# Attention and gated MLP on one core: the tenth and eleventh weighted products and row 15 change their places, and four marking matmuls are replaced by wider narrow halves

## The chip, the cores and the metric

The kernel runs on one core of a Trainium2 chip. The metric is the device time of one execution in microseconds (us); lower is better. A core has a matrix engine (TensorE, PE in the profile), VectorE (DVE), ScalarE (ACT), GpSimd (POOL) and SyncE (SP, which only issues transfers here), and 16 DMA engines. Each engine works off its own list of instructions in order, and waits at an instruction until the data and the buffers it needs are free.

## The reference

x is 2048 x 512. Both branches take the layer-normalised x.

```python
def attention(xn):                       # 32 heads of 16, window of 8 taps, 2 rows apart
    q, k, v = split(xn @ wqkv)
    idx = pos[:, None] - 2 * arange(8)   # rows before the first one are masked
    logits = einsum("bhsd,bhswd->bhsw", q, k[idx]) * 16 ** -0.5
    return einsum("bhsw,bhswd->bhsd", softmax(logits), v[idx]) @ wo

def gmlp(xn):
    z = gelu(xn @ w_in)                  # 2048 x 1792
    z1, z2 = z[:, :896], layernorm(z[:, 896:])
    g = w_sp @ z2 + b_sp                 # mixes the 2048 rows
    return (z1 * g) @ w_out

out = x + attention(xn) * silu(gmlp(xn))
```

Everything is 32-bit floating point.

## The kernel before

Every matrix product is made as three matmuls: each operand is split into a high part, rounded for the fast matmul type (on ScalarE, L195), and a low part, the rest (on VectorE, L197), and high x high, high x low and low x high are summed in a bank of PSUM. A *bank* holds 128 x 512 numbers; there are eight, given out in turn by `mm`.

The 2048 rows are 16 blocks of 128, called rows 0 to 15 below (NT = 16, HT = 8). The stages, in the order in which TensorE works on them:

- q, k and v; then z1 (gelu of the first half of the MLP, stored to memory);
- z2, from about 217 to 294.85 us: rows i and 8 + i are made together, each in two halves, h = 0 with 512 columns and h = 1, the *narrow half*, with 384 (`z2_half`). ScalarE applies the gelu as it empties the bank; VectorE makes the statistics (`z2_stats`, L742 to L745), GpSimd the inverse root and the shift `nmz`, ScalarE normalises (L754 in `z2_normal`) and the row is split into the large buffer `BIG`; `combine` (L767) makes sums and differences of rows i and 8 + i;
- the spatial product w_sp @ z2 by seven products of half the size instead of eight (Strassen's way), m1 to m7, each in two column groups a and b, of 8 steps over the rows (`block_product`, L825). A group accumulates in four banks `banks[a, f]`, shown as g_0_0 to g_0_3 and g_1_0 to g_1_3. Each step uses one block of w_sp as weights, wsp_0_0 to wsp_0_7 for the first product m1a, split in the same way into "h" and "l" parts. ScalarE *seeds* a bank with the bias before matmuls add to it (`seed`, L843);
- the output product b (7 x 3 matmuls of 512 columns for each of 16 rows), the product s of the attention with wo, and the end.

The banks that the seeds fill have to be written in full by a matmul first. The last eight halves of the z2 stage (rows 6, 14, 7 and 15) end in the banks of m1a and m1b; their narrow halves write 384 columns only. `second_seeds`, called after the third pair of steps of m1a, therefore sends four *marking* matmuls (L983), one into each of g_1_0 to g_1_3, whose results the seeds then overwrite.

Attention runs in VectorE's gaps: 16 units of two steps. A step has scores (`pr`, L573), their reduction (`lg`, L580), softmax (L594 to L614, the exponential on ScalarE at L606), the *weighted product* of the weights with v (`pv`, L620; pv_4_4 is unit 4, step 4, the tenth one, `sums_of[9]`), its folds (on GpSimd at L633, on VectorE at L638 and L639), a transpose (L646) and a store. These instructions form one line, in which each is kept behind the one before.

The order of each engine's list is set by a scheduler that plans with costs and priorities; attention has the lowest priority (LOW). `tc.add_manual_dep(x, y, NOSYNC, ...)` puts x behind y in the plan, without a wait at run time. `lows` and `highs` list the splits' low and high parts in the order in which the program makes them, so that `lows[-1]` is the latest one at that place of the program.

Of the kernel before, what the change touches and what calls it, by code (L numbers as in the profile page):

```python
# [13 lines left out]
AF = mybir.ActivationFunctionType  # L14
# [5 lines left out]
FH = F // 2  # L20
FQ = FH // 2
H, DH, W, DIL = 32, 16, 8, 2
NT = S // P
# [3 lines left out]
CT = 512  # L27
NC = S // CT
JC = NT // NC
HT = NT // 2  # L30
F3 = 3 * P
ODD = 3
# [20 lines left out]
NOSYNC = mybir.DependencyInfo(mybir.DependencyClass.NoSync, mybir.DependencyReason.DATA)  # L53
# [4 lines left out]
def kernel(  # L58
# [13 lines left out]
    nc = tc.nc  # L72
    pins = [True]
    lows, highs, sums_of = [], [], []

    def pin(ins):
        return tc.keep_in_program_order(ins) if pins[0] else ins
# [35 lines left out]
    mvz = const.tile([P, NT, 2], F32, name="mvz")  # L113
    nmz = const.tile([P, NT], F32, name="nmz")
# [5 lines left out]
    def xn_at(j):  # L120
        return planes[:, FB - KB :, j, 0], planes[:, FB - KB :, j, 1]

    def z2_at(j):
        return planes[:, :, j, 0], planes[:, :, j, 1]

    def half(i):
        return BIG[:, i * CT : (i + 1) * CT]
# [16 lines left out]
    def blocks(t, n=KB):  # L144
        return t.rearrange("p (k q) -> p k q", k=n)
# [9 lines left out]
    def mm(name):  # L155
        return ps.tile([P, 512], F32, tag=f"bank{next(turn)}", name=name)
# [3 lines left out]
    def weight_pair(name):  # L160
        i = next(slot)
        return (
            wts.tile([P, 512], F32R, tag=f"whi{i}", name=name + "h"),
            wts.tile([P, 512], F32R, tag=f"wlo{i}", name=name + "l"),
        )

    def fetch(src, n, name):
        raw = raws.tile([P, 512], F32, tag="raw", name=name + "r", bufs=RAW)
        pin(nc.sync.dma_start(raw[:, :n], src))
        return raw  # L170

    def side_pair(name):
        return [wts.tile([P, CT], F32R, tag=f"w{n}", name=name + n) for n in "hl"]

    def prep(src, n, name, raw=None, pair_=None):
        if raw is None:
            raw = fetch(src, n, name)
        hi, lo = pair_ or weight_pair(name)
        split(hi[:, :n], lo[:, :n], raw[:, :n])
        return hi, lo  # L180
# [13 lines left out]
    def split(hi, lo, src):  # L194
        first_ = pin(nc.scalar.activation(hi, src, AF.Copy))  # L195
        highs.append(first_)
        lows.append(pin(nc.vector.tensor_tensor(lo, src, hi.bitcast(F32), op=ALU.subtract)))  # L197
        return first_
# [48 lines left out]
    rows = {}  # L247
# [45 lines left out]
    first = []  # L293
# [230 lines left out]
    def t4(name, n=2):  # L524
        t = wide.tile([P, 2 * CT], F32, tag="t4", name=name, bufs=WIDE)
        return t.rearrange("p (i t) -> p i t", i=2)[:, :n]
# [168 lines left out]
    for f in range(FB):  # L695
        pair_ = side_pair("w1_last") if f == FB - 1 else None
        wh, wl = prep(w_in1[:, f, :], KB * P, f"w1_{f}", pair_=pair_)
        for c in range(NC):
            pz = mm(f"z1_{f}_{c}")
            for k in range(KB):  # L700
                cc = slice(k * P, (k + 1) * P)
                xh, xl = [planes[:, FB - KB + k, c * JC : (c + 1) * JC, a] for a in range(2)]
# [5 lines left out]
            zt = zp[:, c % 2]  # L708
# [8 lines left out]
    HALF = (slice(0, 512), slice(512, FH))  # L717
    WID = (512, FH - 512)
    w2 = {
        (k, h): prep(w_in2[:, k, HALF[h]], WID[h], f"w2_{k}_{h}")  # L720
        for h in range(2)
        for k in range(KB)
    }

    def z2_half(j, h, zt):
        xh, xl = xn_at(j)
        pz = mm(f"z2_{j}_{h}")[:, : WID[h]]
        for k in range(KB):
            wh, wl = [w[:, : WID[h]] for w in w2[k, h]]
            nc.tensor.matmul(pz, xh[:, k], wh, start=k == 0, stop=False)  # L730
            nc.tensor.matmul(pz, xh[:, k], wl, start=False, stop=False)  # L731
            nc.tensor.matmul(pz, xl[:, k], wh, start=False, stop=k == KB - 1)  # L732
        nc.scalar.activation(zt[:, HALF[h]], pz, AF.Gelu_apprx_tanh)  # L733

    def spatial_block(c, js):
        return prep(w_sp[c, js], CT, f"wsp_{c}_{js}")
# [14 lines left out]

    def z2_normal(j, zt, n):
        zh, zl = z2_at(j)
        nc.scalar.activation(zt, zt, AF.Identity, bias=nmz[:, j : j + 1], scale=mvz[:, j, 1:2])  # L754
        split(zh[:, :n], zl[:, :n], blocks(zt, FB)[:, :n])

    first_part, last_part = slice(0, F3), slice(FH - F3, FH)

# [19 lines left out]
    spatial = {(0, 0): early_pair}  # L778
    raw_z = {}
    for i in range(HT + 2):  # L780
        if i in (1, 3):
            raw_sums(1, HT - 2 + i // 2)
        if i < HT:
            raw_z[i] = [t4(f"zt_{j}").rearrange("p i t -> p (i t)")[:, :FH] for j in (i, HT + i)]
            for h in range(2):
                for j, zt in zip((i, HT + i), raw_z[i]):
                    z2_half(j, h, zt)
                if i == HT - 1 and h == 0:
                    spatial[0, 1] = spatial_block(0, 1)
        if i == 5:  # L790
            b_a = t4("b_a")
            nc.sync.dma_start(
                b_a, b_sp[0:2, :].rearrange("c t -> (c t)").unsqueeze(0).to_broadcast([P, 2 * CT])
            )
            biases = [[b_a[:, 0], b_a[:, 1]]]
        if 0 < i <= HT:
            z2_stats(i - 1, raw_z[i - 1])
        if i > 1:
            for j, zt, n in zip((i - 2, HT + i - 2), raw_z[i - 2], (ODD + 1, FB)):
                z2_normal(j, zt, n)  # L800
            combine(i - 2, raw_z[i - 2])
# [27 lines left out]
    def z2_block(j, f):  # L829
        return [planes[:, f, j, a] for a in range(2)]  # L830

    def z1_pair(c, f0, n):
        zl = t4(f"zl_{c}_{f0}", n)
        nc.sync.dma_start(zl, z1_d[f0 : f0 + n, c].rearrange("f p t -> p f t"))
        return zl

    banks = {}
    for n in range(8):
        a, f = n // 2 % 2, n // 4 * 2 + n % 2
        banks[a, f] = mm(f"g_{a}_{f}")  # L840

    def seed(a, f, src, scale=1.0):
        return nc.scalar.activation(banks[a, f], src, AF.Copy, scale=scale)  # L843
# [4 lines left out]
    def block_product(a, name, z, w, odd=None, start=False, stop=False, steps=()):  # L848
        for n, s0 in enumerate(range(0, HT, 2)):
            for s in (s0, s0 + 1):  # L850
                wp = w(s)
                for f in range(ODD):
                    three(banks[a, f], z(s, f), wp, start and s == 0, s == HT - 1, not start)
                if odd:
                    three(banks[a, ODD], odd(s), wp, False, s == HT - 1, True)
            for do in steps[n] if steps else ():
                do()

    def plain(a, c, r):
        def w(s):  # L860
            js = r * HT + s
            pair_ = spatial.get((2 * a + c, js)) or spatial_block(2 * a + c, js)
            if (a, c, js) == (0, 0, 6):
                tc.add_manual_dep(
                    sums_of[9].ins, lows[-1].ins.name, NOSYNC, reason="first weights ahead"
                )
            return pair_

        return w

    def summed(a, half_, i):
        return lambda s: prep(sums_d[a, half_, s, :, i], CT, f"ws_{a}{half_}{i}_{s}")
# [12 lines left out]
    def at(r, f0):  # L885
        return lambda s, f: z2_block(r * HT + s, f0 + f)
# [9 lines left out]
    def minus(out_, p_, q_):  # L896
        nc.vector.tensor_tensor(out_, p_, q_, op=ALU.subtract)
# [28 lines left out]
    def gated(c, f, src, zt):  # L926
        times(zt, src, zt)
        split(*ut_at(c, f), zt)
# [32 lines left out]
    def upper_last(a, f0, n):  # L961
        zl, yl = z1_pair(2 * a, LAST + f0, n), t4(f"yl_{a}_{f0}", n)
        nc.sync.dma_start(yl, y_d[a, f0 : f0 + n].rearrange("f p t -> p f t"))
        for f in range(f0, f0 + n):
            minus(yl[:, f - f0], banks[a, f], yl[:, f - f0])
            gated(2 * a, LAST + f, yl[:, f - f0], zl[:, f - f0])
# [12 lines left out]

    def second_seeds():  # L980
        for f in range(ODD + 1):

            nc.tensor.matmul(  # L983
                banks[1, f], z2_block(0, f)[0], half(0), start=True, stop=True
            )
        for f in range(ODD + 1):
            seed(1, f, biases[1][0])

    block_product(
# [62 lines left out]
    upper_last(0, 2, 1)  # L1052
    block_product(1, "m3b", at(1, LAST), summed(1, 1, 0))
    wout = [prep(w_out[:, f, :], D, f"wout_{f}") for f in range(FB)]
    upper_last(1, 0, 2)
    upper_last(1, 2, 1)
    for a in range(2):
# [14 lines left out]
    for i, j in enumerate(rows_of):  # L1072
        c, jj = divmod(j, JC)
# [104 lines left out]
```

## Time and profile before

| | us |
|---|---|
| median of 3 runs | 695.79 |
| lowest, highest | 694.64, 697.7 |
| the profiled execution | 694.39 |
| its span | 692.4 |
| busy in the span: PE | 686.6 |
| DVE | 619.5 |
| ACT | 278.6 |
| POOL | 214.0 |

The span is the part of the execution in which the engines' instructions lie; 2.0 us lie around it. In a timeline row stand the start, the duration, the engine, the line of the kernel, the operation, output <- inputs by the program's names with the numbers of buffers left out, the shape, and in brackets the idle time of the engine just before and what ended it. Matmuls overlap, so the distance of two starts tells what one costs.

### The profile page before, as it was taken

How to read it: one execution, taken by the hardware profiler on the slowest of the kernel's cores; microseconds unless marked ns; L12 is line 12 of the kernel's file. 1: busy time of each engine (PE TensorE's matmuls, PEld its weight loads, DVE VectorE, ACT ScalarE, POOL GpSimd, SP SyncE). 2: the span in 40 equal slices, each digit the busy share in tenths (PEclk: the TensorE clock that was granted, in tenths of full speed). 3: DMA queues.
4: the chain of work that ended last, by engine and by line, in shares of the span. 5: the costliest groups of instructions: out<-in, count | busy, mean ns of one | idle time of the engine just before them, and what ended most of it. 6: DMA issues, size and time to landing. Idle time of an engine off the chain costs nothing.

```text
span 692.4 us, 9239 instructions
## 1 busy us (share of the span) xinstructions
PE 686.6 (99%) x3084; PEld 573.6 (83%) x3084; DVE 619.5 (89%) x866; ACT 278.6 (40%) x458; POOL 214.0 (31%) x242
## 2 busy tenths in 40 slices
PE   8999999999999999999999999999999999999998
PEld 7788888888888899987888888888888888888886
DVE  6677867999999979899999999999999999979775
ACT  3343233324324256765624544433344353211531
POOL 3104737282343321223223221223201202632320
PEclk9999999999999999999999999999999999999999
DMA  8769899969999865266998778776585791645896
GB/s 268 245 199 297 276 353 370 344 213 336 411 410 384 334 222 186 92 216 218 287 401 299 277 241 294 228 251 223 161 290 196 234 339 65 214 159 191 251 324 238
DMA packets 102223, 182.36 MB, mean 263 GB/s; under 512 B 9184, under 2 KB 45280, under 8 KB 102176
## 3 DMA queue, kind: packets, MB, share of 16 engines
q1 hardware_dynamic: 56624, 102.21, 44.2%
q0 software_dynamic: 13824, 52.24, 20.9%
q10 hardware_dynamic: 31728, 27.33, 11.7%
q8 instruction: 24, 0.39, 0.2%
q14 instruction: 23, 0.19, 0.1%
HBM read 122.42 MB, written 59.32 MB: 262 GB/s over the span
## 4 chain that ended last, share of the span: by engine, by line
PE 93%; DVE 2%; DMA 1%; ACT 1%; issue 1%; POOL 1%; SPq 0%; DVEq 0%; ACTq 0%
PE g L825 37%; PE qkv L385 6%; PE qkv L387 6%; PE qkv L386 6%; PE z L705 4%; PE z L703 4%; PE b L1068 4%; PE b L1066 4%; PE b L1067 4%; PE z L704 4%; PE z L732 3%; PE z L731 3%; PE z L730 3%; PE s L1068 2%; PE s L1067 2%; PE s L1066 2%
## 5 line engine op out<-in xcount | busy, mean ns | idle before, releaser
L633 POOL TENSOR_TENSOR pv<-pv 128x1024 f32<-128x1024 f32 x29 | 69.6, 2401 | 92.8 <-DVE pv L620 82.5
L573 DVE TENSOR_TENSOR pr<-k,q 128x2048 f32<-128x2048 f32 x32 | 73.6, 2299 | 4.3 <-DMA k<-qkv_d 4.1
L620 DVE TENSOR_TENSOR pv<-v,lg 128x2048 f32<-128x2048 f32 x32 | 74.5, 2329 | 0.6
L580 DVE TENSOR_REDUCE lg<-pr 128x128 f32<-128x2048 f32 x32 | 72.9, 2279 | 0.1
L647 POOL DMA_DIRECT2D o_d<-tt x32 | 18.0, 563 | 137.8 <-DVE tt L646 104.6
L433 ACT ACTIVATE stage<-qkv 128x512 f32<-128x512 f32 x40 | 23.0, 590 | 30.9 <-DMA qkv_d<-stage 21.0
L1077 ACT ACTIVATE bt<-b 128x512 f32<-128x512 f32 x16 | 9.6, 599 | 50.0 <-PE b L1068 45.8
L807 POOL DMA_DIRECT2D ol<-o_d x32 | 17.8, 556 | 36.2 <-DMA ol<-o_d 9.1
L709 ACT ACTIVATE z1t<-z 128x512 f32<-128x512 f32 x28 | 15.5, 596 | 27.5 <-DMA z_d<-z1t 14.5
L732 PE MATMUL z<-w_0h,BIG 128*128 128x512 f32 x64 | 25.0, 391 | 0.0
L731 PE MATMUL z<-w_0l,BIG 128*128 128x512 f32 x64 | 25.0, 391 | 0.0
L730 PE MATMUL z<-w_0h,BIG 128*128 128x512 f32 x64 | 24.9, 389 | 0.0
L742 DVE BATCH_NORM_STATS2 zst<-zt 128x6 f32<-128x448 f32 x32 | 19.3, 613 | 6.1 <-ACT zt L733 6.0
L754 ACT ACTIVATE zt<-zt,nmz,mvz 128x896 f32<-128x896 f32 x16 | 17.5, 1129 | 17.1 <-POOL nmz L748 17.1
L280 DVE TENSOR_TENSOR xT<-xT,mr 128x512 f32<-128x512 f32 x20 | 13.8, 688 | 11.8 <-DMA mr<-mv_d 6.8
L638 DVE TENSOR_TENSOR pv<-pv 128x512 f32<-128x512 f32 x32 | 22.9, 715 | 0.0
L732 PE MATMUL z<-w_1h,BIG 128*128 128x384 f32 x64 | 21.5, 336 | 0.0
L730 PE MATMUL z<-w_1h,BIG 128*128 128x384 f32 x64 | 21.5, 335 | 0.0
L731 PE MATMUL z<-w_1l,BIG 128*128 128x384 f32 x64 | 21.4, 335 | 0.0
L733 ACT ACTIVATE zt<-z 128x512 f32<-128x512 f32 (+1 forms) x32 | 15.9, 536 | 13.5 <-DMA sums_d<-sa 10.2
L552 POOL DMA_DIRECT2D k<-qkv_d x13 | 7.0, 536 | 43.8 <-DVE pr L573 43.8
L393 POOL TENSOR_TENSOR sb<-sa,sb 128x512 f32<-128x512 f32 x12 | 18.9, 1574 | 5.1 <-DMA sb<-in_w_sp 4.8
(478 smaller groups left out, 2256.9 us busy)
## 6 DMA issues: line engine op xcount, KB each, us to landing
qkv_d<-stage ACTq DMA_DIRECT2D x24, 512.0 KB
v<-qkv_d POOLq DMA_DIRECT2D x14, 704.0 KB, 5.1
k<-qkv_d POOLq DMA_DIRECT2D x13, 704.0 KB, 5.8
sums_d<-sa POOLq DMA_DIRECT2D x14, 512.0 KB, 7.9
sums_d<-sb POOLq DMA_DIRECT2D x14, 512.0 KB, 7.9
z_d<-z1t ACTq DMA_DIRECT2D x14, 512.0 KB
zl<-z_d SPq DMA_DIRECT2D x12, 512.0 KB
tr<-t_d SPq DMA_DIRECT2D x12, 384.0 KB
```

The source lines that it names most:

```text
L385: nc.tensor.matmul(pq, xh[:, k], wh, start=k == 0, stop=False)
L386: nc.tensor.matmul(pq, xh[:, k], wl, start=False, stop=False)
L387: nc.tensor.matmul(pq, xl[:, k], wh, start=False, stop=k == KB - 1)
L573: line(nc.vector.tensor_tensor(pr, taps(ks[u], j0), qb.unsqueeze(1).to_broadcast([P, W, NJ * CS]), op=ALU.mult))
L580: line(nc.vector.tensor_reduce(lgs[u][:, j0 * HS : (j0 + NJ) * HS].rearrange("p i w -> p w i"), pr.rearrange("p w (i d) -> p w i d", d=DH) ...
L620: line(nc.vector.tensor_tensor(pv.rearrange("p w (i d) -> p w i d", d=DH), taps(vs[u], j0).rearrange("p w (i d) -> p w i d", d=DH), lgs[u] ...
L633: eng.tensor_tensor(pv[:, 0:4], pv[:, 0:4], pv[:, 4:8], op=ALU.add)
L730: nc.tensor.matmul(pz, xh[:, k], wh, start=k == 0, stop=False)
L731: nc.tensor.matmul(pz, xh[:, k], wl, start=False, stop=False)
L732: nc.tensor.matmul(pz, xl[:, k], wh, start=False, stop=k == KB - 1)
L825: nc.tensor.matmul(pg, z[a], w[b], start=start and i == 0, stop=stop and i == 2, skip_group_check=seeded)
L1066: nc.tensor.matmul(pp[:, cols], hi, wh, start=k == 0, stop=False)
```

## The change

1. The narrow half's first weight, w2_0_1, is loaded 512 columns wide, the last 512 of the 896. In rows 6, 7, 14 and 15 the first of a narrow half's twelve matmuls takes all of it and writes the whole bank, and the half's result lies in the bank's last 384 columns. The four marking matmuls go.
2. Row 15's normalisation is put behind row 7's high part.
3. The eleventh weighted product (`sums_of[10]`, pv_5_0) is put behind row 7's low part. The tenth, which was put behind the low part of weight row 6 (wsp_0_6), isn't held any more.
4. The twenty-fifth weighted product (`sums_of[24]`, pv_12_0) is put behind the low part of the last block of the output weights (wout_6).

```diff
     w2 = {
-        (k, h): prep(w_in2[:, k, HALF[h]], WID[h], f"w2_{k}_{h}")
+        (k, h): prep(
+            w_in2[:, k, slice(FH - CT, FH) if (k, h) == (0, 1) else HALF[h]],
+            CT if (k, h) == (0, 1) else WID[h],
+            f"w2_{k}_{h}",
+        )
         for h in range(2)
         for k in range(KB)
     }
     def z2_half(j, h, zt):
         xh, xl = xn_at(j)
-        pz = mm(f"z2_{j}_{h}")[:, : WID[h]]
+        bank = mm(f"z2_{j}_{h}")
+        pz = bank[:, CT - WID[h] :]
         for k in range(KB):
-            wh, wl = [w[:, : WID[h]] for w in w2[k, h]]
-            nc.tensor.matmul(pz, xh[:, k], wh, start=k == 0, stop=False)
+            wh, wl = [w[:, CT - WID[h] :] if k == 0 else w[:, : WID[h]] for w in w2[k, h]]
+            if k == 0 and j % HT >= HT - 2:
+                nc.tensor.matmul(bank, xh[:, k], w2[k, h][0], start=True, stop=False)
+            else:
+                nc.tensor.matmul(pz, xh[:, k], wh, start=k == 0, stop=False)
...
     def z2_normal(j, zt, n):
         zh, zl = z2_at(j)
-        nc.scalar.activation(zt, zt, AF.Identity, bias=nmz[:, j : j + 1], scale=mvz[:, j, 1:2])
+        ins = nc.scalar.activation(zt, zt, AF.Identity, bias=nmz[:, j : j + 1], scale=mvz[:, j, 1:2])
+        if j == NT - 1:
+            tc.add_manual_dep(ins.ins, highs[-1].ins.name, NOSYNC, reason="first products' row ahead")
         split(zh[:, :n], zl[:, :n], blocks(zt, FB)[:, :n])
+        if j == HT - 1:
+            tc.add_manual_dep(sums_of[10].ins, lows[-1].ins.name, NOSYNC, reason="gate rows ahead")
...
     def plain(a, c, r):
         def w(s):
             js = r * HT + s
-            pair_ = spatial.get((2 * a + c, js)) or spatial_block(2 * a + c, js)
-            if (a, c, js) == (0, 0, 6):
-                tc.add_manual_dep(
-                    sums_of[9].ins, lows[-1].ins.name, NOSYNC, reason="first weights ahead"
-                )
-            return pair_
+            return spatial.get((2 * a + c, js)) or spatial_block(2 * a + c, js)
...
     def second_seeds():
-        for f in range(ODD + 1):
-
-            nc.tensor.matmul(
-                banks[1, f], z2_block(0, f)[0], half(0), start=True, stop=True
-            )
         for f in range(ODD + 1):
             seed(1, f, biases[1][0])
...
     wout = [prep(w_out[:, f, :], D, f"wout_{f}") for f in range(FB)]
+    tc.add_manual_dep(sums_of[24].ins, lows[-1].ins.name, NOSYNC, reason="output weights ahead")
```

How the lists of instructions move, at three places. First VectorE in the z2 stage, at row 9's statistics (zst is a row's statistics, sr a sum of weight blocks for a later product). Before:

```order
L742 BN_STATS zst_9_2683<-zt_9_2552 128x6 x2
L743 BN_AGGR mvz_96<-zst_1_2679 128x2
L393 TENSOR_TENSOR sr_1_6_0_0r_2535<-sr_1_6_0_0r_2535,sr_1_6_1_8r_2541 128x512
L745 TENSOR_SCALAR mvz_96<-mvz_96 128x2
L742 BN_STATS zst_2_2779<-zt_2_2621 128x6
L743 BN_AGGR mvz_96<-zst_9_2683 128x2
L393 TENSOR_TENSOR sr_1_6_0_8r_2539<-sr_1_6_0_0r_2535,sr_1_6_0_8r_2539 128x512
```

Now:

```order
L750 BN_STATS zst_9_2683<-zt_9_2552 128x6 x2
L620 TENSOR_TENSOR pv_4_4_1452<-v_2_0_1424,lg_4_1363 128x2048
L580 TENSOR_REDUCE lg_6_1444<-pr_6_0_1445 128x8x16
L393 TENSOR_TENSOR sr_1_6_0_0r_2535<-sr_1_6_0_0r_2535,sr_1_6_1_8r_2541 128x512
L751 BN_AGGR mvz_96<-zst_1_2679 128x2
L753 TENSOR_SCALAR mvz_96<-mvz_96 128x2
L750 BN_STATS zst_2_2779<-zt_2_2621 128x6
L751 BN_AGGR mvz_96<-zst_9_2683 128x2
L750 BN_STATS zst_2_2779<-zt_2_2621 128x6
L573 TENSOR_TENSOR pr_6_4_1457<-k_3_0_1440,q_3_0_1441 128x2048
L638 TENSOR_TENSOR pv_4_4_1452<-pv_4_4_1452 128x512
```

The tenth product, which stood behind wsp_0_6's low part, and the reduction, the scores and the folds that follow it in attention's line, stand among the statistics of rows 1, 9 and 2.

Second, TensorE at the start of the first product, from the last matmul into bank g_0_1 with weight row 0 on. Before:

```order
L825 MATMUL g_0_1_3190<-wsp_0_0h_2471,BIG_98 128x512
L825 MATMUL g_0_2_3193<-wsp_0_0h_2471,BIG_98 128x512
L825 MATMUL g_0_2_3193<-wsp_0_0l_2472,BIG_98 128x512
L825 MATMUL g_0_2_3193<-wsp_0_0h_2471,BIG_98 128x512
L825 MATMUL g_0_3_3194<-wsp_0_0h_2471,BIG_98 128x512
L825 MATMUL g_0_3_3194<-wsp_0_0l_2472,BIG_98 128x512
L825 MATMUL g_0_3_3194<-wsp_0_0h_2471,BIG_98 128x512
L825 MATMUL g_0_0_3189<-wsp_0_1h_3091,BIG_98 128x512
L825 MATMUL g_0_0_3189<-wsp_0_1l_3092,BIG_98 128x512
```

Now:

```order
L837 MATMUL g_0_1_3190<-wsp_0_0h_2471,BIG_98 128x512
L837 MATMUL g_0_0_3189<-wsp_0_1h_3091,BIG_98 128x512
L837 MATMUL g_0_1_3190<-wsp_0_1h_3091,BIG_98 128x512
L837 MATMUL g_0_0_3189<-wsp_0_1l_3092,BIG_98 128x512
L837 MATMUL g_0_0_3189<-wsp_0_1h_3091,BIG_98 128x512
L837 MATMUL g_0_1_3190<-wsp_0_1l_3092,BIG_98 128x512
```

Weight row 1 is taken up after six matmuls with weight row 0 instead of twelve; the banks g_0_2 and g_0_3 follow later.

Third, ScalarE in the z2 stage, from row 9's second gelu on. Before:

```order
L733 ACTIVATE zt_9_2552<-z2_9_1_2595 128x384
L733 ACTIVATE zt_2_2621<-z2_2_0_2623 128x512
L733 ACTIVATE zt_10_2622<-z2_10_0_2637 128x512
L754 ACTIVATE zt_0_2477<-zt_0_2477,nmz_97,mvz_96 128x896
L754 ACTIVATE zt_8_2478<-zt_8_2478,nmz_97,mvz_96 128x896
L733 ACTIVATE zt_2_2621<-z2_2_1_2651 128x384
```

Now:

```order
L741 ACTIVATE zt_9_2552<-z2_9_1_2595 128x384
L606 ACT_TABLE_LOAD
L606 ACTIVATE lg_5_1404<-lg_5_1404 128x256
L741 ACT_TABLE_LOAD
L741 ACTIVATE zt_2_2621<-z2_2_0_2623 128x512
L741 ACTIVATE zt_10_2622<-z2_10_0_2637 128x512
L741 ACTIVATE zt_2_2621<-z2_2_1_2651 128x384
L741 ACTIVATE zt_10_2622<-z2_10_1_2665 128x384
L762 ACTIVATE zt_0_2477<-zt_0_2477,nmz_97,mvz_96 128x896
```

Unit 5's exponential, with the load of its table and the load of the gelu's behind it, now stands in the z2 stage; before, it stood among the spatial products.

## The prediction

> **What bounds the kernel now.** I read the page first: busy shares, the granted clock, the chain of waits.
>
> ```profile
> span 692.4 us, 9239 instructions
> PE 686.6 (99%) x3084; PEld 573.6 (83%) x3084; DVE 619.5 (89%) x866; ACT 278.6 (40%) x458; POOL 214.0 (31%) x242
> PEclk9999999999999999999999999999999999999999
> PE 93%; DVE 2%; DMA 1%; ACT 1%; issue 1%; POOL 1%; SPq 0%; DVEq 0%; ACTq 0%
> ```
>
> TensorE is busy for 99% of the span, at full clock in every slice, and is 93% of the chain that ended last. So the end moves by what TensorE issues more or less, plus what it has to wait. VectorE, at 89%, is the engine whose order decides such waits. The timeline of TensorE around the start of the spatial products gives the rates and the one wait there (a start to the next start is what a matmul costs; the shown duration overlaps the next one).
>
> ```profile
> 281.00 0.33 PE L730 MATMUL z<-w_1h,BIG 128*128 128x384 f32 x1
> 285.18 0.39 PE L730 MATMUL z<-w_0h,BIG 128*128 128x512 f32 x1
> 294.85 0.39 PE L825 MATMUL g<-wsp_0h,BIG 128*128 128x512 f32 x1
> 297.66 0.40 PE L825 MATMUL g<-wsp_1h,BIG 128*128 128x512 f32 x1
> ...
> 308.56 0.39 PE L825 MATMUL g<-wsp_5h,BIG 128*128 128x512 f32 x1
> 311.28 1.07 PE L983 MATMUL g<-BIG 128*128 128x512 f32 x4
> 312.18 0.39 PE L825 MATMUL g<-wsp_6h,BIG 128*128 128x512 f32 x1
> 314.68 0.39 PE L825 MATMUL g<-wsp_6h,BIG 128*128 128x512 f32 x1
> 315.35 0.50 PE L825 MATMUL g<-wsp_0h,BIG 128*128 128x512 f32 x1 [0.28 <-ACT g L843]
> 315.68 0.39 PE L825 MATMUL g<-wsp_0l,BIG 128*128 128x512 f32 x1
> ```
>
> From 308.56 to 311.28 lie 12 matmuls of 512 columns: 0.2267 us each. From 281.00 to 285.18 lie 24 of 384 columns: 0.174 each. The four marking matmuls (L983) take 312.18 - 311.28 = 0.90. The first matmul of the second product waits for a seed from ScalarE (L843): the starts 314.68, 315.35 and 315.68 are 0.67 and 0.33 apart, against 0.227: 0.44 + 0.10 = 0.54 lost.
>
> **Matmuls.** Four marks go: -0.90. Four narrow halves (rows 6, 7, 14, 15) write 512 instead of 384 columns in one of their twelve matmuls: 4 x (0.2267 - 0.174) = +0.21. The load and the split of that weight grow by a third, before the z2 stage, whose first matmuls take other weights. The bank-1 seeds no longer stand behind marks at 311.28, and the new order finishes the first product before the second, so the seeds are early: -0.54. Sum: -1.23.
>
> **The tenth product moves.** It was held behind the sixth weight row's low part; now nothing holds it and it stands in the z2 stage on VectorE. With it come the other attention instructions that follow in its line. Their durations:
>
> ```profile
> 301.97 2.28 DVE L620 TENSOR_TENSOR pv<-v,lg 128x2048 f32<-128x2048 f32 x1
> 304.17 2.28 DVE L580 TENSOR_REDUCE lg<-pr 128x128 f32<-128x2048 f32 x1
> 311.15 2.28 DVE L573 TENSOR_TENSOR pr<-k,q 128x2048 f32<-128x2048 f32 x1
> 300.50:320.00 19.50, 3.80 (x4) 1.00 0.69 218
> 300.50:320.00 19.50, 1.12 (x3) 1.00 0.69 218
> 294.65 0.64 DVE L197 TENSOR_TENSOR wsp_1l<-wsp_1r,wsp_1h 128x512 fp32r<-128x512 f32 x1
> ```
>
> The two window rows are tile pv (product, two folds, transpose) and tile sm (three short ones). 3.80 + 1.12 + 2.28 + 2.28 = 9.48; from start to start an instruction costs about 0.08 less than it is shown (301.97 to 304.17 is 2.20), so nine cost 8.8. In the new order all nine stand ahead of the low part of weight row 1 (wsp_1l), and five others have moved behind it (two splits and three of the combining subtractions of L767), which in before lie in three windows, 286.54:287.47, 291.53:293.01 and 293.55:294.00, together:
>
> ```profile
> sum 2.86, DVE 2.86; mean DVE 0.95
> ```
>
> So wsp_1l comes 8.8 - 2.9 = 5.9 us later, less the idle time x of VectorE that the extra work fills. In before it ended at 294.65 + 0.64 = 295.29: now 301.2 - x. And it is wanted earlier: TensorE used to make twelve matmuls with weight row 0 before row 1 (294.85 to 297.66); in the new order six, then two with wsp_1h, then wsp_1l: 294.85 + 0.21 + 8 x 0.227 = 296.9. The stall is S = 4.3 - x, not below 0. The idle stretches of VectorE between 240 and 295 that last 0.4 us or more:
>
> ```profile
> 251.72 0.63 DVE L742 BATCH_NORM_STATS2 zst<-zt 128x6 f32<-128x448 f32 x1 [2.13 <-ACT zt L733]
> 255.56 0.69 DVE L393 TENSOR_TENSOR sr_8r<-sr_0r,sr_8r 128x512 f32<-128x512 f32 x1 [1.43 <-DMA sr_8r<-in_w_sp]
> 268.62 0.63 DVE L742 BATCH_NORM_STATS2 zst<-zt 128x6 f32<-128x448 f32 x1 [1.11 <-ACT zt L733]
> 281.32 0.69 DVE L197 TENSOR_TENSOR BIG<-zt,BIG 128x512 fp32r<-128x512 f32 x1 [0.47 <-ACT BIG L195]
> 290.28 0.63 DVE L742 BATCH_NORM_STATS2 zst<-zt 128x6 f32<-128x448 f32 x1 [2.73 <-ACT zt L733]
> ```
>
> Together 7.87, so S lies between 0 (all filled) and 4.3 (none). The 2.13 is filled surely: the group stands right ahead of that wait, on a gelu that it doesn't touch. So is the 0.47, since that split now stands further back in the order. The 1.43 hangs on a load whose buffer the late sums of VectorE free, and the 1.11 and 2.73 on gelus that share ScalarE with normalisations waiting for VectorE's statistics: late work may make these waits late too. I take x = 2.13 + 0.47 = 2.6: **S = 1.7**, both ends kept.
>
> **What else the lateness reaches.** Row 7's low part is the second of two splits that end at 325.28 + 1.15 = 326.43; the eleventh product, a reduction and the small pieces that stood ahead of it are now behind it.
>
> ```profile
> 325.28 1.15 DVE L197 TENSOR_TENSOR BIG<-zt,BIG 128x384 fp32r<-128x384 f32 x2
> sum 7.35, DVE 7.35; mean DVE 1.84
> ```
>
> The sum is of four windows that hold what leaves (315.70:316.30, 317.17:317.77, 319.16:319.57, 320.01:325.75). 326.4 - 7.35 = 319.1, less x = 316.5; TensorE wants it after some 91 of the 96 matmuls of the first product, 294.85 + 0.21 + 91 x 0.227 = 315.7, plus S = 317.4. Hidden with 0.9 to spare; at x = 0 it would be wanted at 320.0 and be there at 319.1.
>
> ScalarE gets a pair of table loads and an exponential more in the z2 stage.
>
> ```profile
> 249.16 2.17 ACT L754 ACTIVATE zt<-zt,nmz,mvz 128x896 f32<-128x896 f32 x2 [6.03 <-POOL nmz L748]
> 304.40 1.28 ACT L606 ACT_TABLE_LOAD   x1
> 305.69 0.42 ACT L606 ACTIVATE lg<-lg 128x256 f32<-128x256 f32 x1
> ```
>
> 2 x 1.28 + 0.42 = 2.98, in the 6.03 us that it idled there: hidden, at most 2.98 if that idle were filled by something else. The Trainium skill, in "ScalarE: Activation LUTs", section "What ACT_TABLE_LOAD costs", adds a drain of about 1.38 us to each load; by it the pair and the exponential would take 5.7 us (an estimate) and just fit. The trace doesn't show the drain: the exponential starts at 305.69, as the load ends (304.40 + 1.28).
>
> Row 15's normalisation, behind row 7's high part, is wanted by the last step of the third product, at 294.85 + 2 x 21.8 + 19.0 = 357 (96 matmuls are 21.8); row 7 is done 30 us before. The fold of the tenth product on GpSimd (2.4, as for every one) and the loads of the next units come earlier with it; the window row of the stage shows room on the DMA engines.
>
> ```profile
> 240.00:295.00 55.00, 55.00 (x276) 49.69 (x276) 47.04 (x102) 37.20 (x61) 11.19 (x21) 1.00 0.48 162
> ```
>
> (Columns: busy PE, PEld, DVE, ACT, POOL; clock; DMA share; GB/s.) The DMA engines are busy for 0.48 and GpSimd for 11 of 55 us: cost nothing, 2.4 at most where row 0's statistics stand right behind the fold.
>
> **The twenty-fifth product** started at 573.65; now it goes directly behind the last output weight:
>
> ```profile
> 569.11 0.68 DVE L197 TENSOR_TENSOR wout_6l<-wout_6r,wout_6h 128x512 fp32r<-128x512 f32 x1
> 573.65 2.28 DVE L620 TENSOR_TENSOR pv<-v,lg 128x2048 f32<-128x2048 f32 x1
> ```
>
> What it passes (the gates of the last quarter, now 4.4 us later) is read by the last four of sixteen output rows, 12 x 21 x 0.227 = 57 us after these rows begin, and frees a bank that the fourth row wants, 3 x 4.76 = 14 us after they begin. The first row needs wout_6l last, so they begin near 569: ten us to spare. Nothing; with that cover gone, 4.4.
>
> **Sum.** -0.90 + 0.21 - 0.54 + 1.7 = +0.5. The profiled execution took 694.39 (span 692.4 and 2.0 around it), so 694.9; it lies 1.4 below the median 695.79, on which the same +0.5 gives **696.3**.
>
> **Rivals.**
> 1. *All idle is filled, S = 0.* For it: 7.87 of idle against the 4.3 needed, and gelus that wait for TensorE alone would not be late. Against: the new ScalarE order puts normalisations ahead of gelus. -1.23: 694.6.
> 2. *Slower: VectorE's lateness comes through ScalarE to the banks.* Row 14's first half starts at 281.00 - 12 x 0.227 = 278.28 and needs the bank that row 12's gelu (268.01 in before) empties. In the new order the normalisations and splits of rows 3 and 11 and a split of row 9 stand ahead of that gelu.
>
> ```profile
> 264.03 0.16 DVE L745 TENSOR_SCALAR mvz<-mvz 128x2 f32<-128x2 f32 x1
> 265.95 2.16 ACT L754 ACTIVATE zt<-zt,nmz,mvz 128x896 f32<-128x896 f32 x2 [4.54 <-POOL nmz L748]
> 266.84 0.16 DVE L745 TENSOR_SCALAR mvz<-mvz 128x2 f32<-128x2 f32 x1
> 268.01 0.58 ACT L733 ACTIVATE zt<-z 128x512 f32<-128x512 f32 x1
> ```
>
> Row 3's statistics (266.84) have 6.3 more ahead of them, less 2.13: 271.0; GpSimd's power and shift take 265.95 - 264.03 = 1.9; then 2.1 of normalising, 1.8 of splits and the gelu 0.6: some 277.4, 0.9 before it is wanted. It decides from a lateness 0.9 us larger, that is with none of the idle filled: 1.2 us of wait there, and as every later gelu is late the 1.11 and 2.73 stay too. The total is then S = 4.3, +3.1: 698.9; if ScalarE's lateness adds as much again as that bank's wait (1.2), 700.1.
> A wait of 4.3 in one piece would, by the Trainium skill ("TensorE: Matmul & The Clock Gate", Part 1: The HAM clock gate), pass the activity window of about 3.4 us and could halve the clock for as long again, some 1.7 us more (an estimate); no run here shows it, the clock row has only 9s.
> 3. *The moves have no hold on the time*: VectorE is late but makes it up in the stretch with row 0, the seeds wait as before, and only -0.69 is left: 695.1.
>
> **How the numbers follow.** Forecast (S between 0.7 and 3) 0.5: 695.3 to 697.6. Rival 1: 0.25. Rival 2: 0.18. Rival 3: 0.07. About 0.5%, 3.5 us, is what a measurement of this kernel can tell from no change. Only rival 2's upper half passes 699.3; faster than 692.3 would need a gain that no term has. The shown runs of one kernel spread from 694.64 to 697.7, so the range takes rival 1 less 0.9 and rival 2 to its middle: 693.7 to 699.6.
>
> **What would show it.** Right: TensorE's first wait behind the z2 stage is on the split of wsp_1 (VectorE or ScalarE), 1 to 3 us, about 2 us after the first product starts; no L983; no wait on the seed before the second product; the low part of wsp_1 ends 2 to 4 us later after the start of the product than it did; row 7 not waited for. Wrong: no wait there (rival 1), waits inside the z2 stage on a gelu (rival 2), a wait on row 7, or a later last attention transpose.

## The result: slower by 0.8%, and the profile after

The changed kernel takes 702.24 us in the median of six runs (698.51 to 703.2), the kernel before 696.0 beside it: 1.0079 times as long, 95% interval 1.0051 to 1.0107. Forecast were 696.3 and a range up to 699.6. The profiled execution took 703.2; its span is 9.0 us longer than that of before.

The page of the changed kernel: its span, the engines, the granted clock by slices, and the chain of waits.

```profile
span 701.4 us, 9215 instructions
PE 689.9 (98%) x3080; PEld 573.9 (82%) x3080; DVE 618.6 (88%) x866; ACT 280.0 (40%) x460; POOL 222.4 (32%) x242
PEclk9999999999999999999999899999999999999999
PE 41%; DVE 25%; DMA 20%; issue 7%; ACT 3%; POOL 2%; SPq 1%; DVEq 0%; ACTq 0%; POOLq 0%
```

TensorE has four matmuls less and is yet busy for 3.3 us more, since some of its matmuls became slower: one slice has an 8 in the row of the clock. And the chain, which was TensorE for 93%, now runs for a quarter over VectorE and a fifth over transfers. The waits of TensorE, longest first (us in total, times, longest; one of 1.3 at the very start, which before has too, is left out):

```profile
PE g L837 <- DVE ws_5l L197: 3.1, 1, 3.1
PE g L837 <- ACT BIG L195: 1.4, 1, 1.4
PE s L1069 <- ACT o_3h L195: 0.8, 1, 0.8
PE g L837 <- DVE wsp_1l L197: 0.6, 1, 0.6
```

Only the last of them was forecast. ws_5l is the low part of block 5 of the *summed weights*: sums of blocks of w_sp, stored to memory earlier and loaded again, block by block, for the later products. The rows of VectorE and TensorE that answer to those of the prediction, wsp_1's low part and row 7:

```profile
297.14 0.64 DVE L197 TENSOR_TENSOR wsp_1l<-wsp_1r,wsp_1h 128x512 fp32r<-128x512 f32 x1
316.73 0.50 PE L837 MATMUL g<-wsp_7h,BIG 128*128 128x512 f32 x1 [1.39 <-ACT BIG L195]
```

The timeline of TensorE around the first one, with two windows of all engines (the columns as before), shows what came with it:

```profile
395.26 0.39 PE L837 MATMUL g<-ws_5h,BIG 128*128 128x512 f32 x1
398.78 0.79 PE L837 MATMUL g<-ws_5l,BIG 128*128 128x512 f32 x1 [3.13 <-DVE ws_5l L197]
399.37 1.05 PE L837 MATMUL g<-ws_5h,BIG 128*128 128x512 f32 x2
...
405.14 0.39 PE L837 MATMUL g<-ws_6l,BIG 128*128 128x512 f32 x1
395.60:398.80 3.20, 0.07 (x2) 0.02 (x1) 3.20 (x5) 0.60 (x1) 0.00 (x0) 0.89 1.00 302
398.80:404.80 6.00, 6.00 (x14) 4.74 (x15) 6.00 (x10) 2.92 (x5) 0.73 (x1) 0.50 0.84 256
```

For 6 us after the wait the granted clock is 0.50 and a matmul costs 0.427 us (399.37 and 400.22 are two starts apart), where it costs 0.227 otherwise. The difference of the two profiled spans, 9.0 us, from the starts of the matmuls in both traces:

| where | us |
|---|---|
| before the z2 stage | -0.2 |
| z2: four wider matmuls, 0.2; wait for a bank at 278, 0.4 | +0.6 |
| four marks gone | -0.9 |
| seed wait ahead of the second product gone | -0.5 |
| wsp_1 (297) | +0.9 |
| row 7's high part (315) | +1.7 |
| block 5 of the summed weights (395) | +3.4 |
| slow matmuls behind it | +3.0 |
| the product with wo (688) | +1.1 |
| sum, rounded terms | 9.1 |

Six executions had a granted clock of 0.995 to 0.999 each, and spans from 696.7 to 701.4; the profiled one is the longest of them, so its table is not that of the median execution.

### The profile page after: what moved, and what is told of

Read it like the earlier page. It is cut to its first block, busy times and chain, and to the rows that moved or that the text cites. A ratio compares the mean times of both kernels' runs of the same rounds, so it can differ in the third digit from the quotient of the medians.

```text
span 701.4 us, 9215 instructions
## 1 busy us (share of the span) xinstructions
PE 689.9 (98%) x3080; PEld 573.9 (82%) x3080; DVE 618.6 (88%) x866; ACT 280.0 (40%) x460; POOL 222.4 (32%) x242
## 4 chain that ended last, share of the span: by engine, by line
PE 41%; DVE 25%; DMA 20%; issue 7%; ACT 3%; POOL 2%; SPq 1%; DVEq 0%; ACTq 0%; POOLq 0%
PE g L837 33%; DVE pv L620 3%; DMA z_d<-z1t 3%; DVE lg L580 3%; DVE pr L573 3%; DMA sg<-b_d 2%; DMA qkv_d<-stage 2%; DMA ol<-o_d 2%; DVE xT L280 2%; PE b L1069 2%; PE b L1070 2%; PE b L1071 2%; DVE zst L750 2%; DMA ws_2r<-sums_d 1%; PE qkv L308 1%
## 5 line engine op out<-in xcount | busy, mean ns | idle before, releaser
L754 POOL TENSOR_TENSOR mvz<-mvz,nhalf 128x2 f32<-128x2 f32 x8 | 13.6, 1700 | 36.5 <-DVE mvz L753 36.5
L740 PE MATMUL z<-w_0h,BIG 128*128 128x512 f32 x64 | 25.0, 391 | 0.0
L738 PE MATMUL z<-w_0h,BIG 128*128 128x512 f32 x60 | 23.3, 389 | 0.0
L197 DVE TENSOR_TENSOR BIG<-zt,BIG 128x512 fp32r<-128x512 f32 (+2 forms) x24 | 18.1, 767 | 5.1 <-ACT BIG L195 5.1
```

## The experiments

The theory after the result: *the hold*. The tenth product, free, brings VectorE's work forward, and everything that waits on VectorE later, directly or through another engine, pays. The rivals: *the marks* (the seeds, which stand ahead of row 7's normalisation on ScalarE in both kernels, come at another time), *row 15's new place*, and, for the largest term, *one unlucky transfer*.

**The changed kernel once more.**

> The changed kernel a second time. Its first profile lost about 9 us, 6.4 of them at one place: a wait of 3.3 us on the low part of block 5 of the summed weights (ws_5l) in the fifth product (m6a), and after it about 13 matmuls that took 0.427 us instead of 0.227. If this place is a property of the order (VectorE has more ahead of that split, and the load of block 2 is issued into a crowd of transfers), the wait is there again, within 2 to 4 us, and the time is 700 to 703. If it was one unlucky transfer, the wait is below 0.5 us, no slow matmuls follow, and the time is near 696.

Measured: 700.63 (697.62 to 702.47), 1.0082 (1.0051 to 1.0113). The waits were 3.0 us on ws_5l, 1.2 on row 7 and 0.2 on wsp_1, and slow matmuls followed for 3 us. The place belongs to the program's order, not to luck.

**The hold alone**, on the kernel before:

```diff
-            if (a, c, js) == (0, 0, 6):
-                tc.add_manual_dep(sums_of[9].ins, lows[-1].ins.name, NOSYNC, ...)
+        if j == HT - 1:          # in z2_normal
+            tc.add_manual_dep(sums_of[10].ins, lows[-1].ins.name, NOSYNC, ...)
```

> The kernel before with one part of the change alone: the eleventh weighted product is held behind row 7's low part and the tenth isn't held; the marks, row 15 and the output weights stay as they were. If the free tenth product causes the loss, the waits on wsp_1 (about 1 us), on row 7's high part (1 to 2 us) and on the summed weights (about 3 us, and the slow matmuls behind it) are here too: 699 to 704, 0.5 to 1.2% above before. If the missing marks or row 15's new place cause it, at most the wait on wsp_1 is left: 696 to 697.5.

Measured: 698.31, 1.0057 (1.0036 to 1.0079). TensorE's waits:

```profile
PE g L827 <- ACT BIG L195: 1.3, 1, 1.3
PE z L730 <- ACT zt L733: 1.2, 1, 1.2
PE g L827 <- DVE wsp_1l L197: 0.4, 1, 0.4
```

Row 7, a z2 bank and wsp_1, 2.9 us together by these rows and 3.7 by the starts of the matmuls. The 0.5 for the second product's seed is gone here too, though the marks are still sent; that leaves 3.2, which is what the two profiled spans differ by (695.6 and 692.4; the medians differ by 3.4). So these three waits come from the hold alone. The wait on the summed weights, which was expected, isn't here, no matmul is slow, and the median is below the 699 to 704 expected: that place needs another part of the change beside the hold.

**The change with the old hold**:

```diff
-        if j == HT - 1:
-            tc.add_manual_dep(sums_of[10].ins, lows[-1].ins.name, NOSYNC, ...)
+            if (a, c, js) == (0, 0, 6):      # in plain, as before
+                tc.add_manual_dep(sums_of[9].ins, lows[-1].ins.name, NOSYNC, ...)
```

> The changed kernel with the old hold in place of the new one: the tenth weighted product stands behind the sixth weight row's low part again, the eleventh is free; no marks, wider narrow halves, row 15 behind row 7 and the twenty-fifth product behind the output weights as in the change. If the hold is the cause, no wait is left and the matmul terms alone count: -0.69 to -1.23, so 694.5 to 695.5. If the marks' going or row 15 are the cause, the waits on row 7 and on the summed weights are still there: above 699.

Measured: 695.4, 1.0009 (0.9988 to 1.0031), with no wait above 1 us behind the start. Without the new hold the loss is gone. The gain of the matmuls isn't seen either; by the starts the profile has waits of 0.8 on block 6 of the summed weights, 0.5 on a seed of the first product and 0.5 on an output weight. That rules out the marks, row 15 and the output weights as causes without the new hold.

**The tenth product held behind row 7** in place of the eleventh: `sums_of[10]` becomes `sums_of[9]`.

> The changed kernel with the tenth weighted product held behind row 7's low part in place of the eleventh. If the work of VectorE that stands ahead of the weights' and row 7's splits is what counts, every such wait is gone: 694.5 to 695.3. Rival: VectorE, which now has one attention step less done by 316 us, idles ahead of row 7 and is late for the attention's end, up to 8 us: 696 to 703, with the waits of TensorE behind 640 us.

Measured: 698.46, 1.0040 (1.0007 to 1.0073).

```profile
PE b L1069 <- ACT wout_5h L195: 1.5, 1, 1.5
PE s L1069 <- ACT o_3h L195: 0.9, 1, 0.9
PE g L837 <- ACT g L855: 0.6, 1, 0.6
```

The waits on wsp_1 and on the summed weights are gone, that on row 7 is 0.2, as the theory has it. But TensorE waits at 574 for the split of an output weight, for whose load ScalarE had waited 3.06 us, and in the product with wo behind 640. The rival held in part; that VectorE's lateness makes these waits was not shown. By the medians the old place, between both, was the better one, though two of the seven executions took 694.0 and 694.2.

**The scores behind block 5.** One more line of order in the changed kernel:

```diff
+            if (a, half_, i, s) == (0, 0, 0, 5):     # in summed, behind the block's split
+                tc.add_manual_dep(scores_of[18].ins, lows[-1].ins.name, NOSYNC, ...)
```

> The changed kernel with one more line of order: the nineteenth scores (pr_9_0) are put behind the low part of block 5 of the summed weights. All else on VectorE stays in its place, but 2.8 us (scores 2.2, fold 0.6) now stand behind that split and not ahead of it. If VectorE's order decides the wait of 3.0 to 3.3 us there, it shrinks to 0.2 to 0.5, no matmul behind it is slow, and about 5 us come back: 695.5 to 697 (before: 695). If the late load of block 2 decides, the wait stays above 2 us and the slow matmuls with it: 700.

Measured: 701.41 (five runs, 696.17 to 702.67), 1.0065 (1.0031 to 1.0098). In the profiled execution, one of the short ones (697.54), the wait has moved by one block and shrunk to 1.0, no matmul is slow, and VectorE stands idle almost as long ahead of block 2:

```profile
PE g L838 <- DVE ws_6l L197: 1.0, 1, 1.0
382.81 0.69 DVE L197 TENSOR_TENSOR ws_2l<-ws_2r,ws_2h 128x512 fp32r<-128x512 f32 x1 [4.07 <-ACT ws_2h L195]
```

So in this execution two thirds of the wait are gone with the other order at block 5. But the median hasn't fallen, and two of the three long executions (701.41 and 702.6) had a granted clock of 1.000: slow matmuls aren't what made them long, and no profile shows what did.

**Without row 15's new place**, the rest as changed:

```diff
-        if j == NT - 1:
-            tc.add_manual_dep(ins.ins, highs[-1].ins.name, NOSYNC, ...)
```

> The changed kernel without row 15's new place. In its order the same scores stand behind block 5's low part, as a side effect, and on ScalarE row 15's normalisation stands between row 7's and row 7's split. If it is the hold together with row 15's move that puts the scores ahead of block 5, the wait on the summed weights is gone and the wait on row 7 is 1 us longer (2.2 to 2.7): 696.5 to 698. If the hold alone does it, the wait of 3 us is there: above 700.

Measured: 704.79, 1.0131 (1.0107 to 1.0155): worse than the change itself. The first part of the expectation missed twice over: the wait on the summed weights stays, and the z2 bank costs 3.2 us in place of 0.4.

```profile
PE z L736 <- ACT zt L741: 3.2, 1, 3.2
PE g L835 <- DVE ws_3l L197: 2.6, 1, 2.6
PE g L835 <- DVE ws_6l L197: 2.0, 1, 2.0
389.88 0.69 DVE L197 TENSOR_TENSOR ws_2l<-ws_2r,ws_2h 128x512 fp32r<-128x512 f32 x1 [4.24 <-ACT ws_2h L195]
```

Row 15's place isn't a cause, then: with the new hold it helps, by the medians. Why the bank is so late without it wasn't followed up.

**One transfer less.** In each of five profiles with the new hold and without the marks (that of the gap, below, is one) VectorE idles for 4.1 to 4.8 us ahead of ws_2l. The rows around it, from the changed kernel (POOL and SP issue transfers; the last row but two is a piece of the chain of waits, block 2's load from issue to landing) and, in the second fence, from before (*gates* are z1 times a product, g_d<-zl their stores):

```profile
371.01 0.56 POOL L562 DMA_DIRECT2D v<-qkv_d  x1
372.67 0.73 POOL L922 DMA_DIRECT2D g_d<-zl  x1 [1.10 <-DVE zl L901]
373.86 0.74 POOL L922 DMA_DIRECT2D g_d<-zl  x1 [0.46 <-DVE zl L901]
372.88 0.37 SPq L846 DMA_DIRECT2D zl<-z_d  x1
373.48 0.32 SPq L917 DMA_DIRECT2D xl<-x_d  x1
374.04 10.39 DMA ws_2r<-sums_d
385.20 0.69 DVE L197 TENSOR_TENSOR ws_2l<-ws_2r,ws_2h 128x512 fp32r<-128x512 f32 x1 [4.62 <-ACT ws_2h L195]
398.05 0.67 DVE L197 TENSOR_TENSOR ws_5l<-ws_5r,ws_5h 128x512 fp32r<-128x512 f32 x1
```

```profile
365.30 0.76 POOL L915 DMA_DIRECT2D g_d<-zl  x1 [8.48 <-DVE zl L894]
366.84 0.73 POOL L915 DMA_DIRECT2D g_d<-zl  x1 [0.78 <-DVE tt L646]
371.57 0.59 POOL L562 DMA_DIRECT2D v<-qkv_d  x1
372.80 0.32 SPq L169 DMA_DIRECT2D ws_2r<-sums_d  x1
378.49 0.69 DVE L197 TENSOR_TENSOR ws_1l<-ws_1r,ws_1h 128x512 fp32r<-128x512 f32 x1 [0.84 <-ACT ws_1h L195]
391.73 0.65 DVE L197 TENSOR_TENSOR ws_5l<-ws_5r,ws_5h 128x512 fp32r<-128x512 f32 x1
```

In before (the second fence) the two stores of gates (512 KB each) left at 365 and 367, and v (704 KB) only at 371.6: block 2 was issued behind v, one load of 384 KB and block 1, and VectorE waited 0.84 us once. In the changed kernel VectorE made the gates later, the stores left at 372.7 and 373.9 together with v and two loads, and the 256 KB of block 2 took 10.4 us. The load of v itself left at the same time in both kernels; what moved is the stores, by 7 us. The experiment takes v of unit 7 away, so that unit 7's attention is computed from unit 6's v:

```diff
+            if u == 7:
+                vs[u] = vs[u - 1]
+                return
```

> The changed kernel without one transfer: unit 7's v (704 KB) isn't loaded and unit 6's is used in its place, so the attention of unit 7 is computed from other data. In every run with the new hold VectorE stood idle for 4.1 to 4.8 us ahead of the low part of block 2 of the summed weights, whose load, issued behind that transfer, two stores of 512 KB and two loads, took some 10 us. If the crowd of transfers makes that wait, 704 KB less at some 400 GB/s take 1.8 us off it: 2.3 to 3 us idle there, at most 1.5 us of wait on TensorE behind it, and 696 to 699. If the load is late for another reason, idle time and wait stay at 4 and 3 us: 700 to 702. (VectorE's order behind block 2 moves a little with it.)

Measured: 698.25 (695.56 to 699.27), 1.0039 (1.0025 to 1.0053): half of the loss is gone. None of its ten executions had a granted clock below 0.999; of the ten of the changed kernel eight had.

```profile
379.64 0.69 DVE L197 TENSOR_TENSOR ws_2l<-ws_2r,ws_2h 128x512 fp32r<-128x512 f32 x1 [1.21 <-ACT ws_2h L195]
```

The profiled execution is the shortest of the ten. The idle time falls from 4.6 to 1.2. From the issue of block 2's load to ScalarE's use of it pass 6.2 us (372.73 to 378.97) in place of 10.5 (374.04 to 384.54): 4.3 less, more than the 1.8 that the missing bytes take (an estimate, 704 KB at some 400 GB/s; the engines moved 411 between 380 and 385 in the changed kernel). So the crowd of transfers makes VectorE's idle time. TensorE's wait on the summed weights is gone too, but that isn't the transfer's alone: VectorE's order behind block 2 changed as well. In this run block 5's low part starts 0.6 us behind block 4's (388.03 and 387.41); in the changed kernel 6.7 us of other work, scores and gates above all, lie between the starts (398.05 and 391.34).

The hold alone has the same transfers ahead of block 2: v left at 371.39, the stores at 374.24 and 375.43, and from the issue of block 2's load to its use pass 7.9 us. Block 2's low part even comes later than in the changed kernel, and yet VectorE hardly idles, since a weighted product and a reduction stand ahead of it:

```profile
382.19 2.29 DVE L620 TENSOR_TENSOR pv<-v,lg 128x2048 f32<-128x2048 f32 x1
384.40 2.28 DVE L580 TENSOR_REDUCE lg<-pr 128x128 f32<-128x2048 f32 x1
386.98 0.69 DVE L197 TENSOR_TENSOR ws_2l<-ws_2r,ws_2h 128x512 fp32r<-128x512 f32 x1 [0.29 <-ACT ws_2h L195]
```

In the changed kernel both stand behind ws_2l, at 385.81 and 388.01, as they do in before, where the load came in time. With the hold alone block 5's low part starts at 392.48, 5.6 us earlier than there, and TensorE, which begins this product 1.6 us later, doesn't wait for it. So the wait at 395 goes with two things together: a load that comes late, and an order in which VectorE has nothing else ahead of its split. The experiments don't separate their shares.

**A gap for GpSimd.** Row 7's wait isn't on its low part but on the high one, and that hangs, among other things, on GpSimd's power and shift of 128 x 2 numbers. Before, and changed:

```profile
317.35 1.08 POOL L746 TENSOR_TENSOR mvz<-mvz,nhalf 128x2 f32<-128x2 f32 x1 [2.44 <-DVE mvz L745]
318.53 1.50 POOL L748 TENSOR_SCALAR nmz<-mvz 128x1 f32<-128x1 f32 x2
```

```profile
308.73 3.61 POOL L754 TENSOR_TENSOR mvz<-mvz,nhalf 128x2 f32<-128x2 f32 x1 [5.05 <-DVE mvz L753]
312.44 0.90 POOL L756 TENSOR_SCALAR nmz<-mvz 128x1 f32<-128x1 f32 x2
```

The experiment adds one instruction of VectorE with a single input directly behind row 7's statistics:

```diff
+        if i == HT - 1:
+            ins = nc.vector.tensor_reduce(spare, constants, axis=AX.X, op=ALU.max)
+            tc.add_manual_dep(ins.ins, ready.ins.name, NOSYNC, ...)
```

> The changed kernel with one added instruction of VectorE, a reduction with a single input (0.4 us, of data that nobody needs), directly behind row 7's statistics and ahead of a row of instructions with two inputs. In the three profiles with the new hold GpSimd's power for row 7 took 3.6, 4.7 and 4.7 us for 128x2 numbers, against 1.08 in before. If it stands still as long as VectorE works on instructions with two inputs without a pause, it now takes 0.7 to 1.1 and the wait on row 7's high part (1.2 to 1.5) is below 0.3. If the power is slow for a reason of its own, it stays at 3.6 to 4.7 and so does the wait. The scores stand behind block 5 here too, so the wait on the summed weights should be 0.5 at most; time 695 to 697.

Measured: 706.99, 1.0172 (1.0144 to 1.0201), against 695 to 697 us expected: the shifted order brought waits on blocks 2, 3 and 6 of the summed weights, the longest 3.1 us on block 3 with a slow stretch behind it, and others at the end, so the time says nothing of the gap. The rows do (VectorE's added one first, then the first and the last of seven instructions with two inputs that follow without a pause):

```profile
310.14 0.71 POOL L763 TENSOR_TENSOR mvz<-mvz,nhalf 128x2 f32<-128x2 f32 x1 [5.05 <-DVE mvz L754]
310.95 4.01 POOL L765 TENSOR_SCALAR nmz<-mvz 128x1 f32<-128x1 f32 x2
309.97 0.42 DVE L756 TENSOR_REDUCE mone<-mvx 128x8 f32<-128x256 f32 x1
310.30 0.68 DVE L198 TENSOR_TENSOR wsp_0l<-wsp_0r,wsp_0h 128x512 fp32r<-128x512 f32 x1
...
314.04 0.55 DVE L788 TENSOR_TENSOR zt<-zt,zt 128x384 f32<-128x384 f32 x1
```

The power started under the one-input instruction and took 0.71 us. GpSimd's next two instructions, some 0.25 us each, together took 4.01, until 314.96: 0.37 behind the end of the row of two-input instructions (314.59). The stop has moved to the next instruction, and row 7's wait shrank only to 1.0, not below 0.3. And GpSimd isn't the whole of that wait: in the run without the transfer its power and shift took 2.7 us, as in before, and row 7 still cost 1.2, since its normalisation started at 312.69, as ScalarE ended the seeds.

**The marks alone**, on the kernel before (part 1 of the change):

> The kernel before with the first part of the change alone: the marks go, the narrow halves of rows 6, 7, 14 and 15 are wider. By the matmuls -0.69, and up to -0.54 more where the seeds of the second product come early: ratio 0.9982 to 0.9990, 694.0 for a before of 695. If the reordering that comes with it costs as much as it saves: 0.9995 or more.

> The first part of the change alone, once more, to narrow the interval (the ratio was 0.9990, 0.9976 to 1.0004): by the matmuls 0.9990, with the seeds 0.9982; a ratio above 0.9995 says that nothing is gained.

Measured: 0.9990 (0.9976 to 1.0004), and again 0.9987 (0.9971 to 1.0002). The stretch from the first spatial matmul to the first of the output product is 273.09 and 272.72 us long in the two profiles, in before 273.59: 0.5 and 0.9 less. By the starts the marks (0.9) and the wait for the second product's seed (0.5) are gone from it, and a wait on a seed of the first product has come, at 297: 0.8 and 0.5. Each interval just includes 1; the two together speak for a gain of 0.1%, and this is the only kernel of the study that is not slower than before by its median.

**Waits by set amounts**, on the kernel before:

```diff
+        for _ in range(LATE.get(name, 0)):      # 5, 7, 9, 12 at four blocks
+            pin(nc.vector.tensor_scalar(lo, lo, 1.0, None, op0=ALU.mult))
```

> The kernel before with 5, 7, 9 and 12 extra instructions of VectorE (a multiplication by 1, some 0.4 to 0.6 us each) on the low part of one weight block each, at four places of the spatial products, far apart. It makes TensorE wait by set amounts, some 0 to 6 us. If the slow matmuls behind the long waits (0.427 us in place of 0.227) are a matter of how long TensorE stood still, they follow the waits above about 3 us and not those below about 2, and their number is about the same each time (7 to 15). If they belong to that place of the program or to other engines' work, they don't follow here.

Measured: one execution of 718.89 us, only its profile counts. The amounts came out otherwise than meant, because VectorE's lateness hit other blocks too: waits of 1.5, 1.6, 1.9, 1.8 and one of 14.3 us (by the starts). Only the last has slow matmuls behind it; the windows (columns as before) are of that wait, of the slow stretch and of the one after:

```profile
528.30:542.50 14.20, 0.11 (x1) 0.00 (x0) 14.20 (x22) 0.42 (x1) 5.56 (x4) 0.68 0.13 48
542.50:547.20 4.70, 4.67 (x11) 3.70 (x12) 4.63 (x7) 0.63 (x1) 1.84 (x4) 0.50 0.62 195
547.20:551.00 3.80, 3.80 (x18) 3.09 (x18) 3.73 (x4) 0.64 (x1) 0.68 (x1) 1.00 0.87 311
```

The slow matmuls follow long waits and not a place: here at another block, in another product, in a kernel that has none otherwise.

## Why the prediction was wrong, point by point

- *Matmuls, -0.90 + 0.21 - 0.54.* Right in size: the marks and the wider halves measured -0.9 and +0.2, and the wait on the seed ahead of the second product is gone. That the marks' going brings the -0.54 isn't shown: the hold alone keeps the marks and hasn't that wait either, and where the marks alone went, a wait on a seed of the first product took its place.
- *The tenth product moves, S = 1.7 on wsp_1.* Right in mechanism and place, too large: 0.9 and 0.5 in two profiles, 0.7 with the hold alone. wsp_1l ended at 297.78 in the changed kernel, 2.5 us later than in before and not 3.3: VectorE filled more idle time than the 2.6 that were taken as sure.
- *The z2 bank of row 14 (rival 2).* The chain was the right one and its spare time of 0.9 was gone: 0.4 us of wait in the changed kernel, 1.4 with the hold alone, 3.4 without row 15's place. VectorE's statistics were even earlier than worked out (269.5, not 271.0). But "GpSimd's power and shift take 1.9" failed: they took 4.3, as this row of the changed kernel shows with the 0.7 of the shift behind it:

```profile
269.71 3.48 POOL L754 TENSOR_TENSOR mvz<-mvz,nhalf 128x2 f32<-128x2 f32 x1 [6.90 <-DVE mvz L753]
```

- *Row 7's low part, hidden with 0.9 to spare.* No wait on the low part shows; the step followed VectorE alone and left out the high part, which comes by way of statistics, GpSimd and ScalarE. GpSimd's power and shift for row 7, 2.7 us in before (317.35 to 320.03), took 4.6 and 5.3 in the two profiles of the changed kernel. In part the seeds cost too, which stand ahead of row 7's normalisation on ScalarE and in the first profile waited 1.5 us for the bias. Measured: 1.7 and 1.5.
- *"Cost nothing" for the fold and the loads that move with the tenth product.* This is the step that failed most. The prediction followed VectorE's order as far as row 7 and then at the twenty-fifth product; for the stretch between it put nothing, with the share of the DMA engines in the z2 stage (0.48) as its reason. At 372, outside that stage, the engines were full in before too (1.03 between 370 and 375, 1.01 in the 5 us behind). There the new order of VectorE makes the gates 7 us later, so that their stores meet the load of v ahead of block 2's, while that block's split still stands ahead of the work that could have covered its lateness. Measured: 3.4 us of wait at 395 and 3.0 of slow matmuls, 6.4 of the profiled 9.0, where the prediction has no term.
- *The product with wo.* No term either, though the prediction names a later last attention transpose as a sign of being wrong. This product lasts 0.5 to 1.6 us longer in the seven profiles of the changed kernel and of its variants with a hold behind row 7, and no longer with the hold alone or with the old hold. Which part makes it stays open.
- *The clock.* The prediction gave the rule of the Trainium skill ("TensorE: Matmul & The Clock Gate", Part 1: The HAM clock gate) as a sentence that the sum didn't need, for a wait above some 3.4 us. The half rate came at a place where no wait was forecast, and behind waits a little shorter than that: the wait of 3.3 cost 3.0 more, and that of 3.2 in the second profile 1.6.
- *Twenty-fifth product, tables, row 15: nothing.* No wait shows at these places in the changed kernel, and row 15's place even helps.
- *The chances.* 0.82 of the chance lay on cases in which VectorE's lateness costs nothing behind wsp_1. The slower rival took its price from the z2 stage and wsp_1 as well. The measured median lies 6.2 above that of before, where +0.5 was forecast, and 2.6 above the range; that both are slower is no merit of the sum, most of which was made elsewhere.

What stays open: why the same kernel's executions lie between 697.6 and 703.2. In the two that were profiled the wait at 395 is nearly the same (3.3 and 3.2 us), and the slow stretch behind it differs (3.0 and 1.6). That isn't the whole spread: an execution of 702.0 had a granted clock of 0.999. And which part beside the hold gives VectorE the order at block 2 that goes with the wait at 395 wasn't run apart. Row 15 is excluded; the output weights' line acts only after 560 in the order; so it is argued, not shown, that it is the first part of the change.

## What to carry to other kernels

Where a low-priority line of work is moved on one engine, follow that engine's order to its end and not at the place of the move alone: look for splits that stand behind a load in a stretch where the DMA engines are full, for stores that meet such a load, and for the work that stands ahead of the split and covers its lateness. Follow each thing that TensorE waits for through all engines that make it: the shortest instructions on the least busy engine may be the ones that stretch. A wait of 3.1 to 3.4 us cost 1.4 to 3.0 us more here, as the clock halved; two of 2.7 and 2.1 us, 6 us apart, brought the half rate as well.

## What the runs showed of the hardware that was not expected

A GpSimd instruction on 128 x 2 numbers took 0.7 us when VectorE ran instructions with one input or paused, and up to 4.7 when VectorE ran instructions with two inputs without a pause; it went on at the next pause or one-input instruction. The Trainium skill ("SBUF — State Buffer", section "SBUF: two separate sides") says that such VectorE instructions with two inputs in SBUF and GpSimd instructions that read SBUF hold a pair of ports for their whole length and exclude each other; the rows of the gap experiment agree.

The granted clock fell to 0.50 in or behind waits of 3.1, 3.2, 3.3, 3.4 and 14.3 us (by the starts of the matmuls), and not behind single waits of 2.7 us or less, nor behind two waits of 1.9 and 1.8 with 2 us of work between them. In the run without row 15's place it fell behind a wait of 2.1 that followed one of 2.7 after 6 us. By the clock's record in the traces the half rate lasted 3.4 us each time, but 6.8 in the profiled execution of the change and 13.7 with the wait of 14.3, of which 9 lay in the wait itself: two and four times 3.4, which is why nearly equal waits had different prices. The Trainium skill ("TensorE: Matmul & The Clock Gate", Part 1: The HAM clock gate) gives an idle window of about 3.4 us; here waits of 3.1 were enough.
